# Two layers of cached attention and an MLP at batch 8: one score bank and one copy for each head, nine kept value quarters instead of seven

## The chip, the core and the metric

The kernel runs on one core of a Trainium2 chip. The core has a matrix engine (TensorE, PE in the profile), a vector engine (VectorE, DVE), a scalar engine (ScalarE, ACT), GpSimd (POOL) and SyncE (SP), which here issues nearly all DMA transfers. The engines run side by side and wait for each other through semaphores. Tensors lie in the device's memory (HBM); the core computes from its own memory (SBUF, 128 partitions) and from eight matmul result banks (PSUM, 128 partitions x 512 float32 each). The metric is the device time of one execution in microseconds. Before the change it is 1093.52 us, the median of three runs between 1092.39 and 1094.42.

## The reference

Eight tokens (batch rows) pass through two equal layers: attention over a cache, then an MLP.

```python
x = A_x                                        # (8, 1, 448)
x = x + attention(layernorm(x), k_cache, v_cache, wq, wo)
x = x + mlp(layernorm(x), w1, w2, w3, w4)
x = x + attention(layernorm(x), k_cache, v_cache, wq, wo)   # the same caches again
x = x + mlp(layernorm(x), w1, w2, w3, w4)

def attention(x, k, v, wq, wo):                # k, v: (8, 8 heads, 4096, 256) bf16
    q = (x @ wq) as (8, 16 query heads, 1, 256)   # two query heads share a cache head
    p = softmax(q . k / 16)                    # over 4096 positions
    return (p . v) as (8, 1, 4096) @ wo
```

In the MLP the first sublayer shifts by one or two positions of a sequence that has one, so it adds zero; what is left is `x + gelu(layernorm(x) @ w3) @ w4` with normalisations before it. The caches are 134 MB each and are used by both layers. A row's second attention needs the row's whole first layer, since its queries come out of it.

## The kernel before

**Units.** The keys or the values of one row and one cache head are 2 MB. They are cut into four quarters of 512 KB (4 KB for each partition, 1024 positions). `kv` is an area of 30 slots (`QUARTERS`), one quarter each. A load takes one to four neighbouring free slots, and so moves 512 KB to 2 MB (`load`, `issue_kv`; its DMA is issued at line 643).

**Kept quarters.** To read less, some quarters that layer one has loaded for a row stay until layer two has used them: all keys of heads 3 to 6, one quarter of head 7's keys (three more of its quarters are brought back from other places on chip), and `KEEP_V` = 7 quarters of values: all four of head 7 and the last three of head 6 (`KEPT_V`, line 1090). So 24 of the 30 slots can be taken by kept quarters, and six are left as a ring through which everything else passes.

**Order over the rows.** The loop at line 1643 takes row after row. For row b: the MLP of layer one (`mid`), which gives the queries of layer two; then the value part of heads 0 to 2 of row b+1 in layer one, whose keys have been scored ahead; then layer two of row b, heads 6, 7, 5, 4, 3 with kept keys and 0, 1, 2 with keys loaded again; then layer one of row b+1, heads 3 to 7, which fills the kept slots again, and the key part of heads 0 to 2 of row b+2. The passage from the first layer's last head of row b to the second layer's first heads is called the turn of row b below. Through the ring go in a turn twelve value quarters of row b+1, heads 0 to 2, and then the first value quarters of layer two of row b that were not kept, one quarter at a time.

**One head.** `front` (line 1100) makes scores and softmax, `back` (line 1231) the weighted sum of values (PV, line 1257), the product with `wo` (L1307) and, after a layer's last head, the sum for the row. Keys that come fresh are transposed on TensorE (L1476), half a quarter at a time, into one of four banks `psT`, and are copied back to their slot by VectorE (L1407) or ScalarE (L1408), whichever is free in the plan. Scores come in one of two ways. Head 7, and the first head of a row's layer two (head 6), use a matmul for each 128 positions that writes columns directly (L1136). All other heads use rows: `score_rows` (line 1365) takes two quarters, with 32 columns of queries as the weights (all heads of the row, 16 columns, then 16 more), and makes a bank of 4 x 32 partitions x 512 positions in eight matmuls (L1374). `turn_rows` (line 1383) copies this bank to `sr` as bf16 (L1387 on VectorE or L1388 on ScalarE) and turns it with four matmuls against columns of the identity (L1398), which pick the head's two rows of each of the four partition groups, so eight columns each. A head has two such halves: two banks, two copies, eight turning matmuls. There is one `sr`. The queries of layer one lie in `q1b`, those of layer two in `q2T`, two buffers each.

**Order of instructions.** The program does not write its order by hand. `Plan.op` records every operation with what it reads, writes and which bank it uses; `Plan.schedule` is a list scheduler with estimated durations, which fixes the order of each engine and the slots of each load; `synchronise` sets the semaphores. Between estimated gaps it puts matmuls without use ("warm", L1679). Every engine then executes its list in order: SP issues a load when the slot's last reader is done, and all later loads wait behind it. `next_bank` takes the four `psT` banks in turn, past those in `held_banks`, as long as the plan is being written.

Of the kernel before, what the change touches and what calls it, by code (L numbers as in the profile page):

```python
# [6 lines left out]
P = 128  # L7
# [3 lines left out]
DH = 256  # L11
# [8 lines left out]
RSQRT_STEPS = ((0.703952253, 1.681914091), (0.5, 1.5000003))  # L20
RSQRT_F = RSQRT_STEPS[1][0] * RSQRT_STEPS[0][0] ** 3
KEEP_K = 5
KEEP_V = 7
HOLD = 2
MARGIN4, MARGIN2 = 6, 2
REP = 24
# [446 lines left out]
def bass_interleave_layers__gqa_block_cached__mixer_s_mlp__decode_kernel(  # L473
# [42 lines left out]
    w3x_sb = sb("w3x_sb", [P, F // 2], bf)  # L516
    w4_sb = sb("w4_sb", [P, 14 * D], bf)
    ident_f = sb("ident_f", [P, P], f32)
    ident_b = ident_f[:, :].bitcast(bf)[:, 1:2 * P:2]
    xT = sb("xT", [P, NC5, B], bf)  # L520

    x1c = [sb(f"x1c{i}", [P, NC5, 3], bf) for i in range(2)]
# [7 lines left out]
    mask = sb("mask", [P, NC5], bf)  # L530
    mom = sb("mom", [P, 3, B], f32)
    ymk = acc[0]
    cs_q = sb("cs_q", [P, 32], f32)
    cs_h = sb("cs_h", [P, 14], f32)

    mom2 = [sb(f"mom2{i}", [P, 3], f32) for i in range(2)]
# [2 lines left out]
    rsi = sb("rsi", [P, 2, B], i32)  # L539
    rst = rsi[:, :, :].bitcast(f32)  # L540
    rsy = sb("rsy", [P, 2, B], f32)
    q1b = [sb(f"q1b{i}", [P, 48], bf) for i in range(2)]
    lin = sb("lin", [P, 2, 2], f32)
    kh = sb("kh", [P, 1024], bf)
    q2T = [sb(f"q2T{i}", [P, 48], bf) for i in range(2)]
    cursor[0] = (cursor[0] + 31) // 32 * 32
    hb0 = cursor[0]
    NB = 14 * (B - 2)
# [18 lines left out]
    o_row = over("o_row", [B, D], bf, kh)  # L567
    cursor[0] = max(cursor[0], hb0 + 8 * P)
    x_row = over("x_row", [B, NC5 * P], bf, w4_sb)
    NR, NO, NS = 6, 2, 2  # L570
    pT = [sb(f"pT{i}", [P, 32, 2], bf) for i in range(NR)]
# [6 lines left out]
    oT = [sb(f"oT{i}", [P, 2, 2], bf) for i in range(NO)]  # L578
    xs = over("xs", [P, G], f32, pT[0])

    sS = [sb(f"sS{i}", [P, 64], bf) for i in range(NS)]
    oS = sb("oS", [P, 2, DH], bf)
    o_last = over("o_last", [P, G], bf, oS)
    sel = sb("sel", [P, 2], bf)
    self_f = sb("self_f", [P, 2], f32)
# [80 lines left out]
    def const_a(gp):  # L666
        gp.memset(ident_f[:, :], 0.0)
        gp.memset(x_row[:, D:D + P], 0.0)
        gp.memset(mask[:, :], 1.0)
        gp.memset(x3T[:, :, :], 0.0)  # L670
        for q in q1b + q2T:
            gp.memset(q[:, :], 0.0)
        for t, one, minus in [(t, 1, 2) for t in x1c + x2c] + [(xf, 1, 0), (xf, 4, 5)]:
            gp.memset(t[:, :, one:one + 1], 1.0)
            last = gp.memset(t[:, :, minus:minus + 1], -1.0)
        return last
# [413 lines left out]
    KEPT_V = {HKV - 1 - i: range(max(4 * i + 4 - KEEP_V, 0), 4) for i in range((KEEP_V + 3) // 4)}  # L1090
    done = {}

    def first_q(b, prio):
        for c in range(2):
            dv(lambda v, c=c: v.tensor_copy(
                q1b[b % 2][:, 16 * c:16 * c + 16].rearrange("p (h j) -> p h j", j=2),
                psM[:, Q1 + b:Q1 + 32 * B:B].rearrange("p (h j c) -> p h c j", j=2, c=2)[:, :, c, :]),
               rd=["q1"], wr=[("q1b", b % 2, c)], banks=[M], prio=prio)

    def front(layer, b, h, prio=None):  # L1100
# [6 lines left out]
        kept_k, kept_v, banks_of = state.pop((0, b, h)) if layer else ({}, {}, {})  # L1107
        keep_k = KEPT_K.get(h, ()) if layer == 0 else ()
        if layer == 0:
            def rhs(c):  # L1110
                return q1b[b % 2][:, 16 * c + 2 * h:16 * c + 2 * h + 2]
            qall = q1b[b % 2]
            qk = [("q1b", b % 2, 0), ("q1b", b % 2, 1)]
        else:
            def rhs(c):
                return q2T[b % 2][:, 16 * c + 2 * h:16 * c + 2 * h + 2]
            qall = q2T[b % 2]
            qk = [("q2", b % 2, h)]
        ks = dict(kept_k)
        fresh = [u for u in range(4) if u not in ks and not (layer and h == HALF)]  # L1120
        ks.update(load(A_k_cache, b, h, fresh, keep_k))
# [29 lines left out]
        for u in range(4):  # L1151
            full = [("s", ks[u], 0), ("s", ks[u], 1)]

            def of(s, q=ks[u]):
                return slot_ap(q, s * 256, 256)

            def of_kh(s):
                return kh[:, (s % 4) * 256:(s % 4) * 256 + 256]
            if u in fresh:
                for pc in range(2):  # L1160
                    if last_head and layer == 0 and u == 1:
                        half_piece(ks[u], pc)
                        continue
                    bank = transpose_piece(ks[u], pc, u in hold)
                    if u in hold:
                        held.setdefault(u, []).append(bank)
            if last_head and u == 1:
                if layer == 0:
                    score_op(u, range(4), of_kh, ["kh"])
                    o = score_op(u, range(4, 8), of, [("s", ks[u], 1, 0), ("s", ks[u], 1, 1)])  # L1170
                    o.frees = [ks[u]]
                else:
                    score_op(u, range(4), of_kh, ["kh"]).tbank = ["P0", "P1"]
                    half_back()
                    score_op(u, range(4, 8), of_kh, [("khb", 0), ("khb", 1)])
                continue
            if rows:
                if u % 2 == 0:
                    continue
                o = score_rows([ks[u - 1], ks[u]], qall, qk + full + [("s", ks[u - 1], 0), ("s", ks[u - 1], 1)], prio)  # L1180
                turn_rows(u // 2, h, o.tbank, par, prio)
            else:
                o = score_op(u, range(8), of, full)
            if layer and h == first2[b] and u == 3:
                o.hot = False
            if (layer, b, h, u) == (1, B - 1, free_heads[-1], 3):
                o.quiet = True
            if layer and last_head and u == 0:
                for x in (3, 2):
                    for pc, bank in enumerate(banks_of[x]):  # L1190
                        evacuate(ks[x], pc, bank).tbank = bank
                        held_banks.remove(bank)
                continue
            if layer and u == 3 and h == first2[b]:
                lent[b] = ks[u]
            elif rows:
                o.frees = [ks[x] for x in (u - 1, u) if x not in keep_k]
            elif u not in keep_k:
                o.frees = [ks[u]]
# [31 lines left out]
    def back(layer, b, h):  # L1231
# [17 lines left out]
        for u in range(4):  # L1249

            def pv(t, u=u, q=vs[u]):
                last = None
                for s in range(8):
                    i = 8 * u + s
                    g4 = 32 * (i % 4)
                    k = 16 * (u // 2) + 4 * (s % 4) + 2 * (u % 2) + s // 4 if in_rows else i
                    last = t.matmul(ps[g4:g4 + 2, PV0:PV0 + DH], pT[nr][:, k, :],  # L1257
                                    slot_ap(q, s * 256, 256), start=(i < 4), stop=(i >= 28),
                                    skip_group_check=True, tile_position=(0, g4))
                return last  # L1260
# [101 lines left out]
        tcount[0] += 1  # L1362
        return (tcount[0] - 1) % NT

    def score_rows(qs, qall, keys, prio):


        bank = next_bank()

        def mm(t):  # L1370
            last = None
            for c in range(2):
                for g in range(4):
                    last = t.matmul(psT[bank][32 * g:32 * g + 32, :], qall[:, 16 * c:16 * c + 32],  # L1374
                                    slot_ap(qs[g // 2], g % 2 * 1024, 1024)[:, c:1024:2], start=(c == 0),
                                    stop=(c == 1), skip_group_check=True, tile_position=(0, 32 * g))
# [3 lines left out]
        o.tbank = bank  # L1380
        return o

    def turn_rows(half, h, bank, par, prio):

        def ev(e):
            if e is nc.vector:
# [1 line left out]
            return e.copy(sr[:, :], psT[bank][:, :])  # L1388
        plan.op("ev", ev, {"dve": 0.71, "act": 0.6}, "evr", rd=[("psT", bank)], wr=SR, banks=[("T", bank)],
                prio=prio and prio + len(plan.ops)).tbank = bank  # L1390

        picks = ident_b.rearrange("p (g c) -> p g c", g=4)[:, :, 2 * h:2 * h + 2]

        def mm(t):
            last = None
            for k in range(4):
                a = SB + 32 * half + 8 * k
                last = t.matmul(psM[:, a:a + 8], sr[:, k * P:(k + 1) * P], picks, start=True, stop=True)  # L1398
            return last
        plan.op("pe", mm, (0.17, 0.17, 32, 4), "scturn", rd=SR + ["ident_f"],  # L1400
                wr=[("sc", par, x) for x in range(2 * half, 4)], banks=[M], prio=prio and prio + len(plan.ops))

    def evacuate(i, pc, bank):
        def ev(e):
# [116 lines left out]

    def second_queries(b, h, prio):

        q, src = q2T[b % 2], x2c[b % 2]
        pe(lambda t: q_mms(t, range(4 * h, 4 * h + 4), lambda kc: src[:, kc, 0:1], psM, SC,
                           1, QW), 16, rd=[("x2", b)] + WQ, wr=["psM"], banks=[M], prio=prio, width=QW)
        dv(lambda v: v.scalar_tensor_tensor(
            q[:, 0:32].rearrange("p (c x) -> p c x", c=2)[:, :, 2 * h:2 * h + 2],
            cs_q[:, 4 * h:4 * h + 4].rearrange("p (c j) -> p c j", c=2), mom2[b % 2][:, 2:3],
            psM[:, SC:SC + 4].rearrange("p (j c) -> p c j", c=2), ALU.mult, ALU.add),  # L1530
           rd=["psM", ("mom2", b), "cs_q"], wr=[("q2", b % 2, h)], banks=[M], prio=prio)
# [207 lines left out]
```

## Time and profile before

| | |
|---|---|
| time, median of 3 runs | 1093.52 us (1092.39 to 1094.42) |
| profiled execution: time, span | 1095.86 us, 1094.1 us |
| granted TensorE clock, mean | 0.933 |
| busy: PE, DVE, ACT, POOL | 948.4, 665.9, 335.0, 98.0 us |
| read from HBM | 434.18 MB, 397 GB/s over the span |
| SP waiting for a PV (L1257) before a load | 517.7 us, 150 times |
| loads of 2048, 1024 and 512 KB of keys | 69, 3, 40 |
| loads of 2048, 1024 and 512 KB of values | 53, 21, 187 |

A line such as `L1387 DVE CAST sr<-psT ... x157 | 108.4, 691 | 73.6 <-PE psT L1374 60.2` is a group of instructions: kernel line, engine, operation, what it writes and reads, number, then busy time in us, mean ns of one, and idle time of the engine before them with what ended most of it. PEld is the loading of weights into TensorE, which can lie beside a matmul. In the first page's part 2 each digit is the busy tenth of one of 40 slices of the span; the row GB/s is what the DMA engines moved in each slice. "us to landing" is the time from SP's issue of a load to the semaphore that tells that it has arrived; it holds the time in the queue behind earlier loads.

### The profile page before, as it was taken

To read this page: it belongs to the slowest core of one execution; us is meant where nothing else is said; L and a number is where in the kernel's file an instruction comes from. 1 tells how busy PE (TensorE), PEld (TensorE's weight loads), DVE (VectorE), ACT (ScalarE), POOL (GpSimd) and SP (SyncE) were. 2 spreads that over 40 slices of the span, in tenths; PEclk is the share of its full clock that TensorE was granted. 3 is DMA by queue.
4 is the path that set the end of the run, shared out by engine and by line. 5 is a ranking of instruction groups with operands and counts; after the bars stand their busy time and mean duration, and the time that the engine had idled before them with its cause. 6 is when DMAs were issued, how large, how long until landed. Compare 5 with 4: busy or idle time off the path is not lost.

```text
span 1094.1 us, 34653 instructions
## 1 busy us (share of the span) xinstructions
PE 948.4 (87%) x15414; PEld 636.6 (58%) x15414; DVE 665.9 (61%) x2004; ACT 335.0 (31%) x935; POOL 98.0 (9%) x281
## 2 busy tenths in 40 slices
PE   4889888898988989888988889888898998999886
PEld 3556555565556655666556565566555765566554
DVE  3457445675656756666567675667555765566565
ACT  0234123341334303343133322334133440343131
POOL 0001000010100101011010101001010000111010
PEclk9899899997999969999799998999899997999896
DMA  9999999999999999999999999999999999999892
GB/s 333 409 424 421 391 403 425 426 418 375 410 424 427 412 390 392 425 424 415 372 425 425 424 404 390 425 425 420 398 380 427 424 417 381 396 426 410 310 412 120
DMA packets 60417, 436.43 MB, mean 399 GB/s; under 512 B 6494, under 2 KB 9708, under 8 KB 39276
## 3 DMA queue, kind: packets, MB, share of 16 engines
q1 hardware_dynamic: 60260, 434.22, 97.5%
q8 instruction: 121, 1.98, 0.7%
q14 instruction: 28, 0.23, 0.1%
q10 hardware_dynamic: 8, 0.00, 0.0%
HBM read 434.18 MB, written 0.01 MB: 397 GB/s over the span
## 4 chain that ended last, share of the span: by engine, by line
DMA 57%; PE 31%; DVE 6%; ACT 2%; issue 2%; SPq 1%; POOL 0%; POOLq 0%; DVEq 0%
DMA kv<-in_A_v_cache_dram 39%; DMA kv<-in_A_k_cache_dram 15%; PE psT L1476 8%; PE psP L1257 8%; PE psT L1374 4%; PE psM L1136 3%; PE psR L1307 2%; PE psM L892 2%; DMA wqx_sb<-in_A_wq_dram 2%; DMA w_sb<-in_B_w_dram 1%; PE psM L1054 1%; DVE kv L1407 1%; ACT pT L1221 1%; SPq L626 1%; ACT kv L1408 1%
## 5 line engine op out<-in xcount | busy, mean ns | idle before, releaser
L1476 PE MATMUL psT<-ident_f,kv 128*128 128x128 f32 x2752 | 391.5, 283 | 27.0 <-DMA kv<-in_A_k_cache_dram 25.0
L1476 PEld LDWEIGHTS psT<-ident_f,kv 128*128 128x128 f32 x2752 | 296.7, 142 | 111.8 <-issue 69.6
L1407 DVE COPY kv<-psT 128x512 f32<-128x512 f32 x388 | 265.7, 690 | 135.3 <-PE psT L1476 131.4
L1408 ACT COPY kv<-psT 128x512 f32<-128x512 f32 x332 | 193.3, 586 | 437.3 <-PE psT L1476 340.1
L1257 PE MATMUL psP<-kv,pT 128*2 128x256 bf16 x4096 | 185.8, 293 | 36.4 <-DMA kv<-in_A_v_cache_dram 28.8
L1387 DVE CAST sr<-psT 128x512 bf16<-128x512 f32 x157 | 108.4, 691 | 73.6 <-PE psT L1374 60.2
L1257 PEld LDWEIGHTS psP<-kv,pT 128*2 128x2 bf16 x4096 | 76.1, 82 | 90.0 <-DMA kv<-in_A_v_cache_dram 44.3
L1211 POOL PARTITION_ALL_REDUCE gm<-pm x128 | 45.4, 355 | 773.2 <-DVE pm L1209 768.4
L1374 PE MATMUL psT<-kv,q1b 128*32 128x512 bf16 x896 | 72.5, 394 | 17.9 <-ACT kv L1408 14.9
L1221 ACT ACTIVATE pT<-sS,nb,fac 128x32 bf16<-128x32 bf16 x128 | 52.6, 417 | 106.9 <-DVE nb L1215 106.9
L1271 DVE CAST oS<-psP 128x256 bf16<-128x256 f32 x128 | 53.7, 419 | 45.8 <-PE psP L1257 45.3
L1307 PE MATMUL psR<-wo_sb,oT 128*1 128x448 bf16 x444 | 67.4, 387 | 3.5 <-DVE oT L1287 3.1
L1225 POOL PARTITION_ALL_REDUCE Db<-rs x128 | 51.0, 398 | 195.3 <-ACT pT L1221 195.3
L1374 PE MATMUL psT<-kv,q2T 128*32 128x512 bf16 x768 | 60.3, 397 | 3.4 <-DVE kv L1407 2.0
L1398 PEld LDWEIGHTS psM<-ident_f,sr 128*128 128x128 bf16 x832 | 42.5, 97 | 30.7 <-DVE sr L1387 16.5
L1398 PE MATMUL psM<-ident_f,sr 128*128 128x8 bf16 x832 | 52.4, 170 | 7.9 <-DVE sr L1387 6.5
L1221 ACT ACTIVATE pT<-sS,nb 128x32 bf16<-128x32 bf16 x128 | 40.8, 326 | 57.7 <-DVE nb L1215 57.6
L1273 DVE TENSOR_TENSOR oS<-psP,oS 128x256 bf16<-128x256 f32 x128 | 54.2, 424 | 3.5
L1281 PEld LDWEIGHTS psP<-sel,oS 128*128 128x128 bf16 x512 | 24.4, 99 | 39.5 <-DVE oS L1273 29.2
L1204 DVE CAST sS<-psM 128x64 bf16<-128x64 f32 x128 | 27.8, 217 | 29.5 <-PE psM L1136 20.2
L1281 PE MATMUL psP<-sel,oS 128*128 128x2 bf16 x512 | 32.2, 167 | 14.1 <-DVE oS L1273 13.3
L1388 ACT CAST sr<-psT 128x512 bf16<-128x512 f32 x51 | 29.8, 585 | 42.2 <-PE psT L1374 37.9
(197 smaller groups left out, 853.0 us busy)
## 6 DMA issues: line engine op xcount, KB each, us to landing
kv<-in_A_k_cache_dram SPq DMA_DIRECT2D x69, 2048.0 KB, 20.8
kv<-in_A_v_cache_dram SPq DMA_DIRECT2D x53, 2048.0 KB, 17.8
kv<-in_A_v_cache_dram SPq DMA_DIRECT2D x187, 512.0 KB, 7.5
kv<-in_A_v_cache_dram SPq DMA_DIRECT2D x21, 1024.0 KB, 11.1
kv<-in_A_k_cache_dram SPq DMA_DIRECT2D x40, 512.0 KB, 8.1
kv<-in_A_k_cache_dram SPq DMA_DIRECT2D x10, 1536.0 KB, 15.6
kv<-in_A_v_cache_dram SPq DMA_DIRECT2D x5, 1536.0 KB, 12.2
wo_sb<-in_A_wo_dram SPq DMA_DIRECT2D x1, 3584.0 KB, 45.6
```

Of the source, the lines that this page charges most:

```text
L1221: return a.activation(pT[nr][:, :, :].rearrange("p i j -> p j i")[:, jj, :], sview[:, jj, :], ACT.Exp, bias=nb[nm][:, jj:jj + 1], scale=sc ...
L1257: last = t.matmul(ps[g4:g4 + 2, PV0:PV0 + DH], pT[nr][:, k, :], slot_ap(q, s * 256, 256), start=(i < 4), stop=(i >= 28), skip_group_check= ...
L1271: plan.op("dve", lambda v: v.tensor_copy(oS[:, 0, :], po), 0.36, "o", rd=[("pv", par, x) for x in range(4)], wr=["oS0"], banks=[bk], prio=hi)
L1273: plan.op("dve", lambda v: v.tensor_tensor(oS[:, 1, :], po, oS[:, 0, :], ALU.subtract), 0.36, "o", rd=["oS0"] + [("pv", par, x) for x in r ...
L1281: last = t.matmul(ps[:, PV1 + 2 * c:PV1 + 2 * c + 2], oS[:, w, c:DH:2], sel[:, :], start=(w == 0), stop=(w == 1))
L1307: last = t.matmul(psR[r:r + 1, 0:D], oT[no][:, i % 2, i // 2:i // 2 + 1], wo_sb[:, a:a + D], start=(k == 1 and i < 2), stop=(k == turn_at ...
L1374: last = t.matmul(psT[bank][32 * g:32 * g + 32, :], qall[:, 16 * c:16 * c + 32], slot_ap(qs[g // 2], g % 2 * 1024, 1024)[:, c:1024:2], sta ...
L1387: return e.tensor_copy(sr[:, :], psT[bank][:, :])
L1398: last = t.matmul(psM[:, a:a + 8], sr[:, k * P:(k + 1) * P], picks, start=True, stop=True)
L1407: return e.tensor_copy(dst, psT[bank][:, :])
L1408: return e.copy(dst, psT[bank][:, :])
L1476: last = t.transpose(psT[bank][:, s * P:(s + 1) * P], src, ident_f[:, :])
```

## The change

`KEEP_V` goes from 7 to 9: the values kept between the layers are now all four quarters of heads 7 and 6 and the last one of head 5. 26 of the 30 slots are then kept ones, and the ring has four.

The queries of both layers and both buffers move into one tensor `qz`, 16 columns of queries with 16 columns of zeros before and behind each. `score_rows` now takes the half as well: for the first half the window of 32 columns begins at the queries, for the second 16 columns earlier, so that the queries fall on rows 16 to 31 of each group and the zeros on rows 0 to 15. Both halves accumulate into the same bank, in 16 matmuls as before, and the bank is held from the first half to the last. `turn_rows` is called once for a head: one copy, and four turning matmuls with 16 columns each, into the same 64 columns of `psM` in another order, which `back` reads accordingly. Several tensors are allocated in another order.

```diff
-KEEP_V = 7
+KEEP_V = 9
...
+    cs_q = sb("cs_q", [P, 32], f32)
+    qz = sb("qz", [P, 272], bf)
+    kh = sb("kh", [P, 1024], bf)
+    pT = [sb(f"pT{i}", [P, 32, 2], bf) for i in range(NR)]
+    sS = [sb(f"sS{i}", [P, 64], bf) for i in range(NS)]
+    oS = sb("oS", [P, 2, DH], bf)
...
-        for q in q1b + q2T:
-            gp.memset(q[:, :], 0.0)
+        gp.memset(qz[:, :], 0.0)
...
+    def at_q(layer, b, c):
+        return 128 * layer + 64 * (b % 2) + 16 + 32 * c
...
+        def rhs(c):
+            a = at_q(layer, b, c) + 2 * h
+            return qz[:, a:a + 2]
...
-                o = score_rows([ks[u - 1], ks[u]], qall, qk + full + [("s", ks[u - 1], 0), ("s", ks[u - 1], 1)], prio)
-                turn_rows(u // 2, h, o.tbank, par, prio)
+                if u == 1:
+                    rbank = next_bank()
+                    held_banks.add(rbank)
+                o = score_rows([ks[u - 1], ks[u]], u // 2, lambda c, half: at_q(layer, b, c) - 16 * half, rbank,
+                               qk + full + [("s", ks[u - 1], 0), ("s", ks[u - 1], 1)], prio)
+                if u == 3:
+                    turn_rows(h, rbank, par, prio)
...
-                    k = 16 * (u // 2) + 4 * (s % 4) + 2 * (u % 2) + s // 4 if in_rows else i
+                    k = 8 * (s % 4) + 4 * (u // 2) + 2 * (u % 2) + s // 4 if in_rows else i
...
-    def score_rows(qs, qall, keys, prio):
-        bank = next_bank()
+    def score_rows(qs, half, window, bank, keys, prio):
         def mm(t):
             for c in range(2):
+                a = window(c, half)
                 for g in range(4):
-                    last = t.matmul(psT[bank][32 * g:32 * g + 32, :], qall[:, 16 * c:16 * c + 32],
-                                    slot_ap(qs[g // 2], g % 2 * 1024, 1024)[:, c:1024:2], start=(c == 0),
-                                    stop=(c == 1), skip_group_check=True, tile_position=(0, 32 * g))
+                    last = t.matmul(psT[bank][32 * g:32 * g + 32, :], qz[:, a:a + 32],
+                                    slot_ap(qs[g // 2], g % 2 * 1024, 1024)[:, c:1024:2],
+                                    start=(half == 0 and c == 0), stop=(half == 1 and c == 1),
+                                    skip_group_check=True, tile_position=(0, 32 * g))
...
-    def turn_rows(half, h, bank, par, prio):
+    def turn_rows(h, bank, par, prio):
...
-        picks = ident_b.rearrange("p (g c) -> p g c", g=4)[:, :, 2 * h:2 * h + 2]
+        held_banks.remove(bank)
+        picks = ident_b.rearrange("p (g a x) -> p a g x", g=4, a=2)[:, :, :, 2 * h:2 * h + 2]
...
-                a = SB + 32 * half + 8 * k
-                last = t.matmul(psM[:, a:a + 8], sr[:, k * P:(k + 1) * P], picks, start=True, stop=True)
+                a = SB + 16 * k
+                last = t.matmul(psM[:, a:a + 16], sr[:, k * P:(k + 1) * P], picks, start=True, stop=True)
```

More of the change, by code (lines that the diff above doesn't have):

```diff
@@ L518, in bass_interleave_layers__gqa_block_cached__mixer_s_mlp__decode_kernel @@
     ident_f = sb("ident_f", [P, P], f32)
+    NR, NO, NS = 6, 2, 2
     ident_b = ident_f[:, :].bitcast(bf)[:, 1:2 * P:2]
+    cs_q = sb("cs_q", [P, 32], f32)
[4 more added lines that the diff above has]
+    oS = sb("oS", [P, 2, DH], bf)
     xT = sb("xT", [P, NC5, B], bf)
@@ L532, in bass_interleave_layers__gqa_block_cached__mixer_s_mlp__decode_kernel @@
     ymk = acc[0]
-    cs_q = sb("cs_q", [P, 32], f32)
     cs_h = sb("cs_h", [P, 14], f32)
@@ L541, in bass_interleave_layers__gqa_block_cached__mixer_s_mlp__decode_kernel @@
     rsy = sb("rsy", [P, 2, B], f32)
-    q1b = [sb(f"q1b{i}", [P, 48], bf) for i in range(2)]
     lin = sb("lin", [P, 2, 2], f32)
-    kh = sb("kh", [P, 1024], bf)
-    q2T = [sb(f"q2T{i}", [P, 48], bf) for i in range(2)]
     cursor[0] = (cursor[0] + 31) // 32 * 32
@@ L569, in bass_interleave_layers__gqa_block_cached__mixer_s_mlp__decode_kernel @@
     x_row = over("x_row", [B, NC5 * P], bf, w4_sb)
-    NR, NO, NS = 6, 2, 2
-    pT = [sb(f"pT{i}", [P, 32, 2], bf) for i in range(NR)]
     pm = [sb(f"pm{i}", [P, 2], f32) for i in range(NS)]
@@ L579, in bass_interleave_layers__gqa_block_cached__mixer_s_mlp__decode_kernel @@
     xs = over("xs", [P, G], f32, pT[0])
-    sS = [sb(f"sS{i}", [P, 64], bf) for i in range(NS)]
-    oS = sb("oS", [P, 2, DH], bf)
     o_last = over("o_last", [P, G], bf, oS)
@@ L1095, in first_q @@
             dv(lambda v, c=c: v.tensor_copy(
-                q1b[b % 2][:, 16 * c:16 * c + 16].rearrange("p (h j) -> p h j", j=2),
+                qz[:, at_q(0, b, c):at_q(0, b, c) + 16].rearrange("p (h j) -> p h j", j=2),
                 psM[:, Q1 + b:Q1 + 32 * B:B].rearrange("p (h j c) -> p h c j", j=2, c=2)[:, :, c, :]),
@@ L1109, in front @@
         if layer == 0:
-            def rhs(c):
-                return q1b[b % 2][:, 16 * c + 2 * h:16 * c + 2 * h + 2]
-            qall = q1b[b % 2]
             qk = [("q1b", b % 2, 0), ("q1b", b % 2, 1)]
         else:
-            def rhs(c):
-                return q2T[b % 2][:, 16 * c + 2 * h:16 * c + 2 * h + 2]
-            qall = q2T[b % 2]
             qk = [("q2", b % 2, h)]
+        def rhs(c):
+            a = at_q(layer, b, c) + 2 * h
+            return qz[:, a:a + 2]
         ks = dict(kept_k)
@@ L1379, in score_rows @@
                     banks=[("T", bank)], prio=prio and prio + len(plan.ops))
-        o.tbank = bank
+        if half == 0:
+            o.tbank = bank
         return o
-    def turn_rows(half, h, bank, par, prio):
+    def turn_rows(h, bank, par, prio):
         def ev(e):
@@ L1396, in mm @@
             for k in range(4):
-                a = SB + 32 * half + 8 * k
-                last = t.matmul(psM[:, a:a + 8], sr[:, k * P:(k + 1) * P], picks, start=True, stop=True)
-            return last
-        plan.op("pe", mm, (0.17, 0.17, 32, 4), "scturn", rd=SR + ["ident_f"],
-                wr=[("sc", par, x) for x in range(2 * half, 4)], banks=[M], prio=prio and prio + len(plan.ops))
+                a = SB + 16 * k
+                last = t.matmul(psM[:, a:a + 16], sr[:, k * P:(k + 1) * P], picks, start=True, stop=True)
+            return last
+        plan.op("pe", mm, (0.17, 0.17, 64, 4), "scturn", rd=SR + ["ident_f"],
+                wr=[("sc", par, x) for x in range(4)], banks=[M], prio=prio and prio + len(plan.ops))
     def evacuate(i, pc, bank):
@@ L1522, in second_queries @@
     def second_queries(b, h, prio):
-        q, src = q2T[b % 2], x2c[b % 2]
+        src = x2c[b % 2]
         pe(lambda t: q_mms(t, range(4 * h, 4 * h + 4), lambda kc: src[:, kc, 0:1], psM, SC,
@@ L1527, in second_queries @@
         dv(lambda v: v.scalar_tensor_tensor(
-            q[:, 0:32].rearrange("p (c x) -> p c x", c=2)[:, :, 2 * h:2 * h + 2],
+            qz[:, at_q(1, b, 0):at_q(1, b, 0) + 64].rearrange("p (c x) -> p c x", c=2)[:, :, 2 * h:2 * h + 2],
             cs_q[:, 4 * h:4 * h + 4].rearrange("p (c j) -> p c j", c=2), mom2[b % 2][:, 2:3],
```

## The prediction, made before the result was known

> **What bounds the kernel now.** I read the first page, then the kernel in 80 equal stretches, then single DMA issues inside the slow stretches, then the chain of waits over one turn between the layers.
>
> ```profile
> span 1094.1 us, 34653 instructions
> PE 948.4 (87%) x15414; PEld 636.6 (58%) x15414; DVE 665.9 (61%) x2004; ACT 335.0 (31%) x935; POOL 98.0 (9%) x281
> DMA  9999999999999999999999999999999999999892
> GB/s 333 409 424 421 391 403 425 426 418 375 410 424 427 412 390 392 425 424 415 372 425 425 424 404 390 425 425 420 398 380 427 424 417 381 396 426 410 310 412 120
> ...
> DMA 57%; PE 31%; DVE 6%; ACT 2%; issue 2%; SPq 1%; POOL 0%; POOLq 0%; DVEq 0%
> ...
> L1387 DVE CAST sr<-psT 128x512 bf16<-128x512 f32 x157 | 108.4, 691 | 73.6 <-PE psT L1374 60.2
> ...
> L1398 PEld LDWEIGHTS psM<-ident_f,sr 128*128 128x128 bf16 x832 | 42.5, 97 | 30.7 <-DVE sr L1387 16.5
> L1398 PE MATMUL psM<-ident_f,sr 128*128 128x8 bf16 x832 | 52.4, 170 | 7.9 <-DVE sr L1387 6.5
> ...
> L1388 ACT CAST sr<-psT 128x512 bf16<-128x512 f32 x51 | 29.8, 585 | 42.2 <-PE psT L1374 37.9
> ```
>
> The DMA queues hold work through the whole span, and over half of the chain is DMA. The rate is 425 GB/s except in a dip every 130 us, to 372 to 404. Those dips are the turns, where a batch row passes from layer one to layer two. Two stretches of the turn of row 2 and of what follows it, from the view by windows (the columns are PE, PE loads, DVE, ACT, POOL, then granted clock, DMA share, GB/s), and a stretch in the turn of row 4 in which nearly all loads are single quarters:
>
> ```profile
> 376.00:416.00 40.00, 35.76 (x723) 22.80 (x720) 22.51 (x88) 6.86 (x25) 2.85 (x8) 0.79 1.00 388
> 420.00:500.00 80.00, 71.02 (x979) 48.31 (x975) 52.78 (x134) 31.95 (x84) 8.08 (x22) 1.00 1.01 424
> 657.60:671.30 13.70, 12.99 (x293) 8.13 (x295) 6.99 (x27) 2.01 (x7) 0.75 (x2) 0.77 1.03 407
> ```
>
> How far ahead the loads run is in the time from issue to landing. First the ring in the turns of rows 1 and 2 (windows 262 to 276 and 390 to 405), then one issue each: the first load in the turn of row 2 that waits for head 7 of layer two (412.9), the same in row 5 (801.6), and the load at 1037.06, issued when the queue had run dry:
>
> ```profile
> kv<-in_A_v_cache_dram SPq DMA_DIRECT2D x13, 512.0 KB, 6.4
> ...
> kv<-in_A_v_cache_dram SPq DMA_DIRECT2D x11, 512.0 KB, 7.0
> ...
> kv<-in_A_k_cache_dram SPq DMA_DIRECT2D x1, 512.0 KB, 4.3
> ...
> kv<-in_A_k_cache_dram SPq DMA_DIRECT2D x1, 512.0 KB, 4.7
> ...
> kv<-in_A_v_cache_dram SPq DMA_DIRECT2D x1, 512.0 KB, 4.6
> ```
>
> A quarter takes 512 KB at 407 GB/s, 1.29 us, of the queue. So 7.0 us is five quarters in flight, and 4.1 (the lowest, at 1021.10) to 4.7 us is what a lone quarter needs: there the queue has run out and the slots set the pace.
>
> **The change, part by part.** The sum is made against the profiled execution: 1095.86 us, 1094.1 of span and 1.8 around it, 2.3 above the median of 1093.52.
>
> *Traffic.* Eight rows keep two more quarters each: 16 x 1.29 = 20.6 us less DMA. That is no gain by itself. Before, a turn had ring slots for six prefetched quarters; v6.0 and v5.3 (head, quarter) were among the first loaded into them, and waited there for the queries of layer two. After, they wait in kept slots and four can be prefetched. When layer two starts to free slots, the same quarters lie on chip. Loads from there on are tied to the same releases; only the queue is 2.6 us earlier. So a turn gains no more than the first load after these releases had to spare, its time to landing less the lone quarter's (4.35, between 4.1 and 4.6). By row: 0 has 8.4 at 150.99 (cap 2.6); 1 has 7.1 at 282.43 (2.6); 2 has 4.3 (0); 3 has 6.4 at 542.52 (2.05); 4 has 5.6 at 670.97 (1.25); 5 has 4.7 (0.35); 6 has 5.8 at 932.05 (1.45); 7 ran dry (0). Sum 10.3 us; 9.1 with 4.6 and 11.5 with 4.1.
>
> *The ring of four.* In a turn 12 value quarters of the next row pass through the ring. With six slots a round takes 6 x 1.29 = 7.7, so the release after landing is 0.7 us in rows 2 to 6 and 1.3 in row 1, as medians. Four slots allow 5.15 us, and need 4.35 + 0.7 = 5.05 in the median, 5.65 in row 1, with no reserve for a late PV. I stepped through the twelve landings of rows 1 to 6: each the later of the one before plus one quarter, and the landing four back plus that slot's own release plus the lone latency. It loses 1.5, 0.1, 1.1, 0, 0.5, 0.1 us by row with 4.1 and 2.4, 0.8, 1.9, 0.3, 1.1, 0.7 with 4.6: 3.2 to 7.2 us together, 5.2 taken from the middle. It costs once, since the queue and the PVs between the MLP steps are late together. Behind SP's wait for a late slot stand all later loads (SP issues in order), and behind PE's wait for a late V the MLP and the second queries. SP's waits for slots are 517.7 us in all for L1257 alone, hidden wherever loads have 12 us or more to landing.
>
> *One copy a head.* 208 copies at L1387 and L1388 become 104: 54 us less of DVE and 15 of ACT. 832 turning matmuls become 416, of 16 columns instead of 8: with 52.4 and 42.5 us for both halves of their work, some 45 us less PE. The 16-column form is not in the trace; between nothing more and the 48-column score matmul's 0.04 us apiece at L1136 it stays below 17 us of that. Nearly all of this lies where loads have 12 to 30 us to landing, so it is worth 0 there. From the last K of head 7 to head 7's second scoring, the heads (7, then 6 and 7) do not use rows at all. Only heads 5, 4 and 3 of layer two just after it free K slots a copy (0.69) or less sooner: 0 to 0.5 us a turn, 0 to 4 in all. I take 0, as their loads already have 7 us or more.
>
> *The bank held* from a head's first scoring to its last leaves three for transposes: 0.5 us of PE for four, 0.69 of copy and some 0.35 of hand-offs make 1.55, a piece each 0.52 us against 0.62 that half a 2 MB load's quarter takes at 424 GB/s. It costs 0 while that holds; above it, the weight loads of transposes now idle 111.8 us, of which 69.6 are issue and 37.2 DMA; the 5 left, doubled, bound it: 0 to 5 us, 0 taken.
>
> *Rest.* The scores' matmuls stay 16 per head and width 512; the accumulation in one bank adds none. The four zero fills become one, at the start, where PE waits 13.2 us for POOL's identity: 0 to 0.5 us gained, 0 taken. Addresses move; I see no row that prices them, and take 0, between -1 and 1. The planner makes all orders anew; neighbouring turns of one plan differ by 0.1 to 1.9 us above, so -3 to 3 over the eight, 0 taken.
>
> Sum: 1095.86 - 10.3 + 5.2 = 1090.8 in the profiled execution, 4.9 to 5.1 less, and 1093.5 - 4.9 = 1088.6 as a median.
>
> The Trainium skill, DMA: Bandwidth & Descriptors, section Anatomy of one DMA, fits a transfer of the GpSimd path as 2.0 us plus its bytes at 436 GB/s; an estimate from that page is 3.2 us for 512 KB. By that a ring of four would need 3.9 us, lose nothing, and the sum would end near 1083. The trace differs: 4.1 at least on this queue.
>
> **The rivals.**
> (1) *The ring of four starves; slower.* Place: each turn, from the second head of the next row's values to head 6 of layer two. It decides once the loss passes 10.3 us, 0.12 us for each of 7 x 12 quarters: a round of 5.64, that is, a mean release of 1.3 us, which row 1 has now. With 4.7 + 1.3 = 6.0 it is (6.0 - 5.15) / 4 x 84 = 18 us lost, 8 slower, 1102; with the four quarters behind them too, 24 lost, 1107. For it: single releases of 1.7 to 2.0 us in rows 1 and 3, and PE at a granted 0.6 to 0.8 in the turns. Against it: medians of 0.7 in four rows.
> The Trainium skill, Perfetto Trace Analysis, on consistent bubbles, reads a gap that recurs on the engine that should be full as a sign of too little buffer space; the dips every 130 us agree, and by that rule two slots fewer speak against this change.
> (2) *The whole cut shows.* If the queue, not the releases, paced every turn, 20.6 us would go: 1073. For it: 1.00 of DMA share even in the dips. Against: 4.3 and 4.7 us to landing, and the dry queue at 1035.
> (3) *Nothing moves:* gains and losses within 2 us of each other, 1093.
>
> **How the numbers follow.** A measurement of this kernel tells a change from about 0.2%, 2.2 us. The sum's own case has 0.42, with 1081 to 1091 as its range (9.1 - 7.2 to 11.5 - 3.2, and 4 from the copies). The whole cut has 0.07, no change 0.13, starving 0.38, since its threshold is one that the present kernel already shows in one turn. Faster is 0.49, same 0.13, slower 0.38. The range for 8 in 10 runs from 1077 to 1106: it leaves out the whole cut and the far end of starving.
>
> **What would show it.** HBM read falls from 434.18 to 425.8 MB; copies to sr number 104; L1398's matmuls 416. In the turns single quarters land 4.1 to 5 us after issue, instead of 6 to 7. The dips stay as deep or deepen, while the stretches between keep 424 GB/s: the time between equal landings of neighbouring rows falls by about 0.6 us. Wrong if PE's waits for V at L1257 (73 us now, both rows) grow by over 10 us, or if stretches between the turns fall below 420 GB/s, which would blame the bank or the pieces of loads.

## The result, and the profile after

The changed kernel takes 1101.83 us (median of 4 runs, 1100.83 to 1102.76) against 1092.95 us of the kernel before beside it: a ratio of 1.0088, 95% interval 1.0068 to 1.0109. It is slower by 9 us, where 5 us less was forecast. The rival in which the ring of four starves had said 1102. The profiled execution took 1102.43 us with a span of 1100.5.

From the first page of the changed kernel:

```profile
span 1100.5 us, 33986 instructions
PE 962.7 (87%) x15144; PEld 655.6 (60%) x15144; DVE 598.4 (54%) x1897; ACT 339.0 (31%) x938; POOL 98.3 (9%) x278
DMA  9999999999999989999999999999999999999794
GB/s 322 408 425 423 388 352 426 424 413 348 374 423 426 421 318 414 426 426 407 321 425 425 424 381 369 425 425 418 357 398 426 424 383 322 421 423 397 290 373 165
HBM read 425.80 MB, written 0.01 MB: 387 GB/s over the span
L1392 DVE CAST sr<-psT 128x512 bf16<-128x512 f32 x52 | 36.0, 692 | 30.3 <-PE psT L1377 30.1
L1393 ACT CAST sr<-psT 128x512 bf16<-128x512 f32 x52 | 30.5, 586 | 58.6 <-PE psT L1377 56.9
```

The work that was to go is gone: 8.4 MB of reads, and half of the copies to `sr` (52 and 52, where 157 and 51 stood). Yet the span is 6 us longer. The rate between the turns is what it was, 425 GB/s; the dips are deeper: the lowest slice of a turn is at 318 to 369, where it was at 372 to 391 (rows 0 to 6). PE is busier by 14 us although turning costs less: the turning matmuls go from 52.4 to 26.8 us, but the planner now puts in 426 matmuls without use where 280 were, 87.9 us instead of 56.4. They are meant for gaps that it foresees. They are not what makes the kernel slower: the run below with one copy and seven kept quarters has 406 of them and takes the time of the kernel before.

The two stretches of the turn of row 2 from the view by windows (same columns as before: PE, PE loads, DVE, ACT, POOL, granted clock, DMA share, GB/s):

```profile
376.00:416.00 40.00, 33.68 (x690) 21.92 (x688) 19.77 (x81) 7.59 (x26) 2.67 (x7) 0.87 0.93 346
394.00:411.00 17.00, 16.20 (x346) 10.02 (x350) 7.30 (x44) 0.21 (x1) 0.00 (x0) 0.70 0.88 290
420.00:500.00 80.00, 72.18 (x976) 50.69 (x968) 44.33 (x123) 31.80 (x85) 8.31 (x22) 0.96 1.01 425
```

In the 40 us around the turn the rate falls from 388 to 346, in its inner part to 290, with a DMA share of 0.88: for part of a turn the DMA engines have nothing to do. Before, the share of this stretch was 1.00 in the 40 us and 1.01 from 389 to 405. After the turn it is 425 as before (424).

How long a quarter takes from issue to landing, single value quarters in the turn of row 4, first the kernel before (649.5 to 656.5), then the changed one (657 to 666):

```profile
kv<-in_A_v_cache_dram SPq DMA_DIRECT2D x6, 512.0 KB, 7.1
```

```profile
kv<-in_A_v_cache_dram SPq DMA_DIRECT2D x6, 512.0 KB, 5.7
```

The prediction let four slots work if this fell to 4.4 us. It fell to 5.7 only, and the quarters came further apart.

From the landing times of single loads I worked out three numbers for each turn: the pace of the twelve value quarters of the next row (last landing less first, by 11; mean of rows 2 to 7), and, counted from the landing of head 7's first key quarter, when the first keys of layer two (row 1 to 5, head 0) are issued and when they land (means).

| kernel | kept, ring | us, median | pace, us a quarter | issued after | landed after |
|---|---|---|---|---|---|
| before | 7, 6 | 1093.0 | 1.28 | 38.1 | 43.7 |
| changed | 9, 4 | 1101.8 | 1.61 | 37.8 | 45.2 |

So the ring lost 11 x 0.33 = 3.6 us in a turn. The issue that waits for layer two's scoring came no later than before (37.8 against 38.1 us): the chain through the MLP did not suffer. But its load, which was to find a queue 2.6 us emptier, found a fuller one: 7.0 to 8.0 us to landing in rows 1 to 5, where 4.3 to 7.1 had been. The ring's quarters were issued late and stood in front of it. Landing is 1.5 us later a turn, and the following 68 quarters take 85.3 instead of 86.0 us (both as means of rows 1 to 5). Counted over the first six rows, a row takes 130.98 us instead of 130.26. Six rows make 4.3 us of the 6.4 between the profiled spans; 0.9 is there before the first turn's values land, and the last row's turn with all behind it gives the rest (5.1 more to the last load's landing, 4.0 less from there to the end).

### The profile page after: what moved, and what is told of

Its sections match the earlier page's. It is cut to its first block, busy times and chain, and to the rows that moved or that the text cites. A ratio compares the mean times of both kernels' runs of the same rounds, so it can differ in the third digit from the quotient of the medians.

```text
span 1100.5 us, 33986 instructions
## 1 busy us (share of the span) xinstructions
PE 962.7 (87%) x15144; PEld 655.6 (60%) x15144; DVE 598.4 (54%) x1897; ACT 339.0 (31%) x938; POOL 98.3 (9%) x278
## 4 chain that ended last, share of the span: by engine, by line
DMA 54%; PE 38%; DVE 4%; SPq 1%; issue 1%; ACT 1%; POOL 0%; DVEq 0%
DMA kv<-in_A_k_cache_dram 34%; DMA kv<-in_A_v_cache_dram 19%; PE psT L1481 15%; PE psP L1261 7%; PE psT L1377 5%; PE psM L1135 2%; PE psR L1311 2%; PE psP L1684 1%; DMA w3x_sb<-in_B_w_dram 1%; PE psM L890 1%; PE psM L1052 1%; DVE oS L1277 1%; SPq L642 1%; DVE oS L1275 1%; SPq L625 1%
## 5 line engine op out<-in xcount | busy, mean ns | idle before, releaser
L1481 PE MATMUL psT<-ident_f,kv 128*128 128x128 f32 x2752 | 382.4, 286 | 33.8 <-DMA kv<-in_A_k_cache_dram 31.8
L1481 PEld LDWEIGHTS psT<-ident_f,kv 128*128 128x128 f32 x2752 | 308.4, 145 | 116.7 <-issue 59.7
L1413 ACT COPY kv<-psT 128x512 f32<-128x512 f32 x338 | 197.2, 587 | 411.7 <-PE psT L1481 320.1
L1261 PE MATMUL psP<-kv,pT 128*2 128x256 bf16 x4096 | 183.1, 294 | 24.6 <-DMA kv<-in_A_v_cache_dram 22.7
L1377 PE MATMUL psT<-kv,qz 128*32 128x512 bf16 x1664 | 135.5, 403 | 4.4 <-ACT kv L1413 2.0
L1261 PEld LDWEIGHTS psP<-kv,pT 128*2 128x2 bf16 x4096 | 84.4, 84 | 73.2 <-DMA kv<-in_A_v_cache_dram 30.7
L1275 DVE CAST oS<-psP 128x256 bf16<-128x256 f32 x128 | 54.0, 422 | 52.4 <-PE psP L1261 50.4
L1684 PE MATMUL psP<-ident_f 128*128 128x256 bf16 x356 | 65.0, 305 | 0.0
L1377 PEld LDWEIGHTS psT<-kv,qz 128*32 128x32 bf16 x1664 | 35.0, 96 | 39.6 <-issue 13.1
L1392 DVE CAST sr<-psT 128x512 bf16<-128x512 f32 x52 | 36.0, 692 | 30.3 <-PE psT L1377 30.1
L1135 PEld LDWEIGHTS psM<-qz,kv 128*128 128x128 bf16 x1344 | 43.0, 101 | 15.6 <-issue 4.4
L1135 PE MATMUL psM<-qz,kv 128*128 128x48 bf16 x1344 | 49.9, 190 | 2.6 <-DVE kv L1412 2.0
```

Source lines behind the costliest of these rows:

```text
L1135: last = t.matmul(ps[:, SB + 2 * i:SB + 2 * i + 2 * REP], a()[:, c:256:2], bcast(rhs(c), REP, 1), start=(c == 0), stop=(c == 1))
L1275: plan.op("dve", lambda v: v.tensor_copy(oS[:, 0, :], po), 0.36, "o", rd=[("pv", par, x) for x in range(4)], wr=["oS0"], banks=[bk], prio=hi)
L1377: last = t.matmul(psT[bank][32 * g:32 * g + 32, :], qz[:, a:a + 32], slot_ap(qs[g // 2], g % 2 * 1024, 1024)[:, c:1024:2], start=(half == ...
L1413: return e.copy(dst, psT[bank][:, :])
L1481: last = t.transpose(psT[bank][:, s * P:(s + 1) * P], src, ident_f[:, :])
L1684: return t.matmul(dst, ident_b, bcast(ident_b[:, 0:n // 4], 4, 1), start=True, stop=True)
```

## The experiments

**Theory A**: the ring of four starves in each turn; the scores' half of the change is off the path. **Theory B**: the bank held from the first scoring to the last, or the new plan around it, is what costs. One half alone, each way:

```diff
-KEEP_V = 9
+KEEP_V = 7
```

> The change's score half alone: one bank and one copy for each head, seven kept value quarters, so a ring of six. Theory A (the ring of four starves; the copies lie off the path): 1088 to 1094 us, the twelve value quarters of a turn land 1.28 us apart again, copies to sr number 104. Theory B (the bank held from a head's first scoring to its last, with three banks left for transposes, or the new plan around it, is what costs): 1099 us or more, as with the whole change.

Measured: 1091.14 us against 1092.46, ratio 0.9993, interval 0.9973 to 1.0014. No difference, with the bank held and half of the copies gone. The pace is 1.32 us a quarter. From its page:

```profile
HBM read 434.18 MB, written 0.01 MB: 398 GB/s over the span
L1392 DVE CAST sr<-psT 128x512 bf16<-128x512 f32 x60 | 41.5, 691 | 32.9 <-PE psT L1377 32.7
```

The other half alone, in the kernel before:

```diff
-KEEP_V = 7
+KEEP_V = 9
```

> The other half alone: two banks and two copies as before, nine kept value quarters, ring of four. Theory A: 1099 to 1106 us, the twelve value quarters of a turn land about 1.6 us apart, HBM read 425.8 MB. Theory B: 1073 to 1091 us, since 20.6 us of traffic are gone and the scores are as before.

Measured: 1101.67 us, ratio 1.0081, interval 1.0061 to 1.0101; pace 1.60. This is the whole loss of the change. Theory B falls, both times by its own numbers.

One step between, in the changed kernel:

```diff
-KEEP_V = 9
+KEEP_V = 8
```

> One copy for each head, eight kept value quarters, ring of five. Theory A: five slots allow a round of 6.45 us, and the rounds of the changed kernel take 6.4 to 6.9, so about 1.3 to 1.35 us for a quarter: 1088 to 1096 us. Theory B: 1099 us or more.

Measured: 1091.66 us, ratio 0.9994, interval 0.9977 to 1.0012; pace 1.36. A ring of five nearly holds the pace, and the 4.2 MB less just pay for what is lost.

The ring without the saving, in the kernel before:

```diff
-QUARTERS = 30
+QUARTERS = 28
```

> The kernel before with 28 slots instead of 30: seven kept value quarters, ring of four, traffic as before (434.2 MB). It separates the ring from the traffic saved. Theory A: the twelve quarters of a turn land about 1.6 us apart, and the queue has 2.6 us more to load in each turn than with nine kept, 8 x 2.6 = 20 us over the time with nine kept: 1115 to 1125 us. If the traffic saved brings nothing (as in my step on spare time), it is 1100 to 1108. Theory B: 1093 to 1099 us.

Measured: 1118.83 us, ratio 1.0246, interval 1.0223 to 1.0268; pace 1.66. Two slots fewer cost 26 us; two more kept quarters in the same ring (the run above with nine kept and two copies) give back 1118.8 - 1101.7 = 17 us of the 20.6 that their traffic takes. So in a ring that starves the cut is worth most of its size, 1.07 us for each of 16 quarters. The change pays 26 to get 17.

Single loads in these two, in the turn of row 4 (nine kept, 654 to 662.3; 28 slots, 667.5 to 677.3):

```profile
kv<-in_A_v_cache_dram SPq DMA_DIRECT2D x6, 512.0 KB, 5.9
```

```profile
kv<-in_A_v_cache_dram SPq DMA_DIRECT2D x6, 512.0 KB, 6.1
```

One step the other way:

```diff
-KEEP_V = 9
+KEEP_V = 6
```

> One copy for each head, six kept value quarters, ring of seven; HBM read 438.4 MB. If a ring of six is full already (12 quarters 1.28 to 1.32 us apart), a seventh slot brings nothing and the 4.2 MB more cost 8 x 1.29 = 10 us less what the loads of layer two had to spare: 1094 to 1102 us. If rings of six starve too, 1085 to 1091 us.

Measured: 1099.26 us, ratio 1.0055, interval 1.0038 to 1.0071; pace 1.33. The seventh slot adds no pace; the traffic costs 7 us.

**Why four slots are too few.** A round of a slot is the time to landing and the time until it is issued anew. Theory C: the landing itself takes over 5 us once other loads are in flight. Theory D: a quarter needs 4.1 to 4.7 us as I had taken it, and PE's late releases are what breaks the ring. I measured the loads by themselves. The loop is shortened: `quarter(i)` stands for the address of a quarter, and between two depths SP waits until all has landed.

```python
for depth in (1, 2, 3, 4, 5, 6, 8):
    for i in range(40):
        s = i % depth
        if i >= depth:
            eng.wait_ge(sems[s], 16 * count[s])      # the load before it in this slot has landed
        eng.dma_start(kv[:, s * 2048:(s + 1) * 2048], quarter(i)).then_inc(sems[s], 16)
        count[s] += 1
```

> No attention at all, only the disputed cost: SP loads 512 KB quarters of the values into a ring of 1, 2, 3, 4, 5, 6 and then 8 slots, 40 loads each, and waits only for the landing of the load in the same slot (the output is zeros, all computation is left out). Theory C (a load lands when the slowest of the 16 DMA engines is done, and needs over 5 us as soon as others are in flight, so four slots can't fill the queue whatever the release): about 4.3 us a load at depth 1, over 1.4 at depth 4, 1.28 only from depth 5 or 6. Theory D (a lone quarter needs 4.1 to 4.7 us and the late release by PE is what breaks the ring of four): 4.3, 2.2, 1.45 us at depth 1, 2, 3 and 1.28 from depth 4 on.

The view by windows inside the seven depths, in this order (DVE, POOL, granted clock, DMA share, GB/s), and the issues in the same windows:

```profile
5.00:155.00 150.00, 0.00 (x0) 0.00 (x0) 1.00 0.41 133
165.00:250.00 85.00, 0.00 (x0) 0.00 (x0) 1.00 0.68 221
262.00:328.00 66.00, 0.00 (x0) 0.00 (x0) 1.00 0.85 271
340.00:388.00 48.00, 0.00 (x0) 0.00 (x0) 1.00 0.99 371
398.00:443.00 45.00, 0.00 (x0) 0.00 (x0) 1.00 1.02 407
453.00:498.00 45.00, 0.00 (x0) 0.00 (x0) 1.00 1.03 407
508.00:553.00 45.00, 0.00 (x0) 0.00 (x0) 1.00 1.02 407
```

```profile
kv<-in_A_v_cache_dram SPq DMA_DIRECT2D x38, 512.0 KB, 3.9
kv<-in_A_v_cache_dram SPq DMA_DIRECT2D x36, 512.0 KB, 4.7
kv<-in_A_v_cache_dram SPq DMA_DIRECT2D x35, 512.0 KB, 5.7
kv<-in_A_v_cache_dram SPq DMA_DIRECT2D x34, 512.0 KB, 5.6
kv<-in_A_v_cache_dram SPq DMA_DIRECT2D x34, 512.0 KB, 6.4
kv<-in_A_v_cache_dram SPq DMA_DIRECT2D x33, 512.0 KB, 7.7
kv<-in_A_v_cache_dram SPq DMA_DIRECT2D x31, 512.0 KB, 10.2
```

The pace by landings is 3.97, 2.39, 1.90, 1.41, 1.28, 1.28, 1.28 us a load. With four slots and a release at once (0.02 us) the queue is not full: 371 GB/s, though the DMA share reads 0.99, so the share alone would not tell. It is full from five. The time to landing is 3.9 us for a load that is alone, as I had it, but 4.7 with two and 5.6 to 5.7 with three and four, while the queue still has idle time. Theory D falls: it had 1.45 at depth 3 and 1.28 at depth 4. Theory C's paces hold from depth 4 on; its "over 5 us as soon as others are in flight" holds with two others, not with one. In the kernel a slot is released some 1.0 us after landing, and (5.6 + 1.0) / 4 = 1.65 us, against 1.61 measured. So of the 0.33 us lost for each quarter the landing alone makes 1.41 - 1.28 = 0.13, in a ring that is released at once; the rest needs the release too, for which a landing of 5.6 us leaves no room.

The Trainium skill, DMA: Bandwidth & Descriptors, section Latency and other measured facts, says that the memory's access latency, the main part of a transfer's fixed cost, grows with the load on the memory. The run agrees in its direction, 3.9 to 5.6 us; that the memory is the cause no run here shows.

**Does the order of PE's list matter?** The planner assumes 4.0 us from issue to the start of a transfer's share of the queue. I planned the changed kernel with 5.5:

```diff
-    ISSUE, LEAD = 4.0, 5.0
+    ISSUE, LEAD = 5.5, 5.0
```

> The changed kernel, planned with 5.5 us instead of 4.0 from SP's issue to the start of a transfer's share of the queue; the work is the same, only the order of the engines' lists and the slots change. Theory D (slots are released late because PE's list has the PVs too early or too late for the true landing): 1088 to 1096 us, releases of 0.7 us. Theory C: the ring's pace stays at 1.5 us or more for a quarter, 1097 to 1106 us.

Measured: 1105.87 us, ratio 1.0119, interval 1.0094 to 1.0144; pace 1.76. PVs that stand later in PE's list release later, 1.3 to 4.4 us after landing in the inner part of the turns, and the loads' own time stays: in the turn of row 4

```profile
kv<-in_A_v_cache_dram SPq DMA_DIRECT2D x6, 512.0 KB, 5.8
```

The same with a ring of five (`KEEP_V = 8`):

> One copy for each head, eight kept value quarters (ring of five), planned with 5.5 us from issue to transfer instead of 4.0. Its twelve quarters took 1.36 us apiece with 4.0. Theory D: 1.29 us apiece, some 5 us less than with 4.0: 1083 to 1088 us. Theory C: 1.33 to 1.4 apiece, 1089 to 1095 us.

Measured: 1095.60 us, ratio 1.0029, interval 1.0010 to 1.0048; pace 1.47. Neither theory's pace; later releases (1.6 to 3.2 us in the inner part of the turns before rows 4 to 7) hurt a ring of five as well. Release does count, only not as what was wrong. So the other way, with 3.0 us and a ring of five:

> One copy for each head, eight kept value quarters (ring of five), planned with 3.0 us from issue to transfer instead of 4.0, so that PE's list has the PVs of the turn earlier and slots are released sooner after landing, at the price of PE waiting for values more often. With 4.0 the quarters took 1.36 us apiece, with 5.5 1.47. If release is what is left: 1.29 to 1.32 apiece and 1084 to 1090 us. If PE's waits eat it: 1091 to 1097 us.

Measured: 1102.27 us, ratio 1.0098, interval 1.0072 to 1.0124; pace 1.39. That is outside both expectations: the first keys of layer two land 43.7 us after head 7's, as early as in the kernel before, so its loss lies behind them, and its cause stays open. One sign is in the waits: PE waits 79 us for values (L1261), where it waits 54 in the same ring with 4.0. And with 2.5 us in the changed kernel:

> The changed kernel planned with 2.5 us from issue to transfer instead of 4.0. By the loads alone four slots can do no better than 1.41 us a quarter, even if released at once; with releases of 0.5 to 0.7 it is 1.5 to 1.55 instead of 1.61: 1 us less in each of seven turns, 1092 to 1099 us; 1101 or more if PE's waits for values eat it.

Measured: 1107.62 us, ratio 1.0148, interval 1.0123 to 1.0173; pace 1.59, releases of 0.5 to 1.2 us for most quarters. The pace gains 0.02 us and the kernel loses 6: the keys of layer two are issued 40.4 us after head 7's keys instead of 37.8, so the chain of the turn is longer, and PE stands before values that are not there yet.

Who waited for DMA, from the view of waits (us in total, times, longest), in this run and then in the changed kernel:

```profile
PEld psP L1261 <- DMA kv<-in_A_v_cache_dram: 54.5, 71, 2.8
PEld psT L1481 <- DMA kv<-in_A_k_cache_dram: 54.1, 54, 4.1
PE psP L1261 <- DMA kv<-in_A_v_cache_dram: 38.6, 54, 2.3
PE psT L1481 <- DMA kv<-in_A_k_cache_dram: 37.3, 46, 3.8
```

```profile
PEld psT L1481 <- DMA kv<-in_A_k_cache_dram: 46.7, 50, 2.4
PE psT L1481 <- DMA kv<-in_A_k_cache_dram: 31.8, 40, 2.1
PEld psP L1261 <- DMA kv<-in_A_v_cache_dram: 30.7, 51, 2.3
PE psP L1261 <- DMA kv<-in_A_v_cache_dram: 22.7, 39, 2.2
```

PE's wait for values rises from 53 to 93 us. Both directions of the planner's estimate made these kernels slower; nothing tried here beats the kernel before.

**Loads or bytes?** The loads alone once more, with a ring of 2 MB and one of 3 MB cut into pieces of 1 MB, 512, 256 and 128 KB:

> Loads alone again, each issued when the load before it in its slot has landed (output zeros, all computation left out): 16 MB each through a ring of 2 MB cut into 2 loads of 1 MB, 4 of 512 KB, 8 of 256 KB, 16 of 128 KB, and then the same for a ring of 3 MB (3, 6, 12, 24 loads). If the landing by the slowest DMA engine is a fixed lateness of some 4 us for each load, what counts is how few bytes wait for it: per 512 KB about 2.4 us (1 MB loads), 1.41 (512 KB), 1.28 to 1.33 (256 KB), 1.3 to 1.4 (128 KB, with smaller packets) at 2 MB, and 1.28 to 1.4 at 3 MB from 512 KB down. If only the bytes in flight count, all cuts of 2 MB take about 1.41.

The eight windows in the order 2 MB (four cuts) and 3 MB (four cuts), same columns as above:

```profile
5.00:48.00 43.00, 0.00 (x0) 0.00 (x0) 1.00 0.95 363
54.00:96.00 42.00, 0.00 (x0) 0.00 (x0) 1.00 0.99 371
102.00:144.00 42.00, 0.00 (x0) 0.00 (x0) 1.00 1.05 379
150.00:205.00 55.00, 0.00 (x0) 0.00 (x0) 1.00 0.89 272
214.00:250.00 36.00, 0.00 (x0) 0.00 (x0) 1.00 1.01 423
256.00:294.00 38.00, 0.00 (x0) 0.00 (x0) 1.00 1.02 407
300.00:342.00 42.00, 0.00 (x0) 0.00 (x0) 1.00 1.05 378
348.00:405.00 57.00, 0.00 (x0) 0.00 (x0) 1.00 0.89 273
```

Per 512 KB: 1.45, 1.44, 1.37, 1.92 us at 2 MB and 1.24, 1.28, 1.35, 1.90 at 3 MB. In pieces of 1 MB and of 512 KB the bytes in flight count, not the loads: 2 MB is too little in both cuts, even as two loads of 1 MB, which I had at 2.4 us, and 3 MB is faster in both. The finer cuts do not separate the two readings. Pieces of 256 KB run at 378 to 379 GB/s in either ring, with the DMA engines full (share 1.05) and packets of half the size; that the packets are the reason is not shown. Pieces of 128 KB run at 272 to 273 in either ring because SP issues only one in 0.47 us: in these two windows it never waits for a slot. In 2 MB the pieces of 256 KB are a little faster than quarters, 1.37 against 1.44 us; an estimate from this for a finer ring of four slots is 11 x 0.07 x 7 = 5 us at most, less than the 9 that the change lost. No kernel was tried with it.

## Why the prediction was wrong

*The ring of four* is the step that failed. It had the right place and the right form, a round of four slots, and the wrong term: a lone quarter's 4.1 to 4.6 us as time to landing, taken from issues at moments when the queue was nearly or wholly dry. They were not loads alone: before the one at 1021.10 (4.1 us) three had yet to land, but these had been issued 4.1 to 6.5 us earlier. In the changed kernel's ring of four the three others have been issued within the last 5 us (1.61 us apart), and the time is 5.6 to 5.7 us, in the loads alone as in the kernel. With 5.6 us in its place, the prediction's own stepping through the twelve landings, with the releases of the kernel before, loses 2.3 to 4.4 us by row, 3.2 in the mean. Measured is a loss of 0.33 us for each of 11 quarters, 3.6 us a turn, where I had 0.5 to 1.2 as the mean of rows 1 to 6. Over seven turns it is 25 us instead of 5.2, and the run with 28 slots has 26. The trace of before had a row that would have warned: no stretch of it ran four deep at full rate. The turn of row 1 kept 1.27 us a quarter at 5.9 to 6.4 us to landing, 4.6 to 5 quarters in flight; that is as shallow as the trace shows a full queue, and I went below it by means of a number from an empty one. The release of 0.7 us, read as the median of rows 2 to 6, was too small for two of them: slot by slot it is 0.9 in row 2 and 1.1 in row 3. That is the smaller part; the changed kernel's 1.0 is 0.3 above what I took, its landing 1.25 above.

*Traffic.* The cap by spare time, 10.3 us, holds only where the ring is full. The run with one step (ring of five) got 4.2 MB less for nothing, as the cap and a small loss would have it. In a starving ring the two quarters that no longer pass it are worth more, 17 us. The forecast of what the first load of layer two would meet was wrong in its sign: the queue was later, not earlier.

*One copy a head* and *the bank held*, each taken at 0, were right in their sum: 0.9993, interval 0.9973 to 1.0014. One run holds both, so that each is 0 by itself is not shown. That the releases of layer two stay where they were (37.8 against 38.1 us) was right as well.

*Starving as a rival* had its threshold at a round of 5.64 us and a price of 8 us for a round of 6.0. The round was 4 x 1.61 = 6.4, for which the same formula gives 27 us of loss and 1110 us. The traffic gave back 17 us and not 10.3, so that 1102 was met is partly luck: loss and gain were both larger than the rival had them. The Trainium skill, Perfetto Trace Analysis, on consistent bubbles, was the better guide here: the dips grew with each slot taken away (the lowest of the slices 10 to 37 is 372 GB/s with six slots, 360 with five and one copy, 318 in the changed kernel). By the fit that the prediction took from the Trainium skill, DMA: Bandwidth & Descriptors, section Anatomy of one DMA, a ring of four had 1.2 us to spare; the loads alone show that it has none.

*What would show it*: reads, copies and matmuls came out as written; single quarters did not land in 4.1 to 5 us but in 5.7; the stretches between the turns kept 425 GB/s; PE's waits for values did not grow (73 to 53 us) although the kernel was slower; that this is so because the plan put the PVs later was not tried by itself. The time from row to row rose by 0.7 us, where a fall of 0.6 was forecast.

## What to carry to other kernels

The time to landing of a load issued into an empty queue does not tell how few buffers can keep the queue full; look in the trace for the shallowest stretch that still runs at full rate, and take that product of time and rate (here 5 quarters, 2.5 MB) as the least. Buffers taken from a stream to hold data save traffic one for one, but below that least each one costs time on every load that passes. When a change joins two edits, run each alone first: here one was worth nothing and the other was the whole loss.

## What the runs showed that I had not expected

The time to landing rises with load well before the queue is full: 3.9, 4.7, 5.7 us with one, two and three loads in flight, at 133, 221 and 271 GB/s.

In the changed kernel the DMA engines do not run dry together. In row 2's turn four quarters of the next row were issued by 387.2 and landed at 393.98, 395.25, 396.53 and 397.82; one more was issued at 394.46. In the five microseconds from 392 the DMA share and the rate were

```profile
392.00:393.00 1.00, 0.77 (x14) 0.27 (x14) 0.61 (x3) 0.00 (x0) 0.00 (x0) 1.00 0.95 373
393.00:394.00 1.00, 0.00 (x0) 0.00 (x0) 0.67 (x3) 0.00 (x0) 0.00 (x0) 1.00 0.72 287
394.00:395.00 1.00, 0.81 (x18) 0.47 (x18) 0.29 (x2) 0.00 (x0) 0.00 (x0) 1.00 0.43 172
395.00:396.00 1.00, 0.70 (x20) 0.48 (x20) 0.04 (x1) 0.00 (x0) 0.00 (x0) 1.00 0.58 164
396.00:397.00 1.00, 1.00 (x22) 0.43 (x18) 0.17 (x1) 0.00 (x0) 0.00 (x0) 0.80 0.97 324
```

From 394 to 395 over half of the engines' time was idle while three of the four had yet to land. A load counts as landed with the last of 16 updates of its semaphore, and the trace has the time of each: for the load that landed at 395.25 the first came at 390.43, 4.8 us earlier, and for the other two it was as early. So parts of a load are done long before the whole.

This unevenness is not what makes the 5.6 us in the loads alone. There, by the same updates, the first comes 2.7 us after the issue with one load in flight and 4.3 with four (medians), and from the first to the last it takes 1.2 and 1.0 us; only with two and three in flight is the spread wider, 2.0 and 2.1. In the kernels' rings it is 3.0 us before and 2.1 in the changed kernel (the six loads of row 4 above). Why it is wider there no run shows.
